# Another written order for the steps of a fused attention and SoLU kernel

## The chip, the cores and the metric

The kernel runs on one core of one Trainium2 chip. The metric is the device time of that core in microseconds (us): 400.5 us before, the median of three runs (400.12 to 400.53). The core has five engines that work side by side, each through its own queue in order: TensorE (PE in the profile; its weight loads PEld), VectorE (DVE), ScalarE (ACT), GpSimd (POOL) and SyncE (SP), which here issues all the transfers to and from memory.

## The reference

Packed attention for 8 batches of 8 heads, then a SoLU layer on the result:

```python
def sm_attn(qq, kk, vv):
    s = scale * np.matmul(qq, kk.transpose(0, 1, 3, 2))
    a = np.exp(s - np.max(s, axis=-1, keepdims=True))
    a = a / (np.sum(a, axis=-1, keepdims=True) + 1e-09)
    return np.matmul(a, vv)
p_packed = sm_attn(p, k, v)            # p: (8, 8, 32, 64), k, v: (8, 8, 576, 64)
out = sm_attn(q, p_packed, p_packed)   # q: (8, 8, 576, 64)
x = out.transpose(0, 2, 1, 3).reshape(4608, 512)
h = x @ w_in                           # w_in: 512 x 1024, float64
e = np.exp(h - np.max(h, axis=-1, keepdims=True))
solu = h * e / (np.sum(e, axis=-1, keepdims=True) + 1e-09)
mu = np.mean(solu, axis=-1, keepdims=True)
var = np.mean((solu - mu) ** 2, axis=-1, keepdims=True)
return ((solu - mu) / np.sqrt(var + 1e-06) * g_ln) @ w_out   # w_out: 1024 x 512, float64
```

## The kernel before

The work is cut into flows, each a Python generator. One step of a flow records the few instructions up to its next `yield`. The flows are:

- `Z`: warm-up matmuls on TensorE that feed nothing (L115, L117).
- loads, all issued by SP: `lw0` to `lw3` and `lo0` to `lo3` (1024 KB each, a quarter of w_in or of w_out, L168), `lg` (g_ln, L174), `lp` (p in two parts, 128 and 384 KB, L189), `lk`, `lq` and `lv` (one batch of k, q or v).
- `W0` to `W3` and `O0` to `O3` turn the float64 words of the weights into float32: a pass over the high words on ACT (L221), a shift on DVE (L223), a pass over the low words on ACT (L234), an add on POOL (L242, L254). `O` also sums squares on ACT (L251), for which it needs `g`, the transposed g_ln (PE L178, ACT L180). `S` and `C0` to `C7` split w_out into two fp16 parts `wch` and `wcl`.
- `p` transposes p on TensorE (L201) and copies it out on ACT (`pT`, L207).
- `k0` to `k7` (`pack`) make the packed attention of a batch: the transposed `kT`, scores (L385), exponentials (ACT L393), their transposes (L423, copied to `e1T` by ACT L425), the product with v (L433), and `ppT` (L440, L443). For batches 0 and 1, k and q are transposed by TensorE (L355, L361); for the later ones by DVE (L368).
- `q0` to `q7` (`unpack`) make the second attention of a batch: scores (L496, L505), softmax on all four engines, and the fp16 halves `a_h`, `a_l` (for batch 0 `a_r`, ACT L519 and DVE or POOL L521).
- `z0` to `z7` multiply the packed result by w_in (L565, L559) and split it into `zh`, `zl`. x @ w_in is then formed as attention weights times z.
- `t0` to `t35`: token tiles of 128 rows. A tile is 12 matmuls of 512 columns into `h` (L633; 24 of half height for a tile that lies across two batches), then max (DVE L636), exponential (ACT L654), product (DVE L658), centred halves `yhl` (ACT L664, DVE L666), a transpose by DMA (L669, `yT`), 24 matmuls of 512 columns with w_out (L688), a scaling (DVE L693) and the store (L695).

The steps run in the order of one string, and nothing reorders them afterwards:

```python
for name in ORDER.split():
    next(flows[name], None)
```

So the string sets, for each engine, the order of its queue. A load also waits for its buffer: `raw` has three, and `zh` and `zl` have two each, which first hold the raw words of weights. `LOAD_IN` says which weight goes where: lw2, lw0, lo1, lo3 into `zh`, lw1, lw3 into `zl`, lo0, lo2 into `raw`. A TensorE step that writes `h` waits for one of three pairs of PSUM banks.

Of the kernel before, what the change touches and what calls it, by code (L numbers as in the profile page):

```python
# [754 lines left out]
```

## Time and profile before

| | before |
|---|---|
| median of the runs | 400.5 us (400.12 to 400.53) |
| the profiled execution's own time | 401.95 us |
| its span, from the first to the last instruction | 400.2 us |
| PE busy | 383.8 us (96%) |
| DVE busy | 300.4 us (75%) |
| ACT busy | 259.4 us (65%) |
| POOL busy | 249.1 us (62%) |
| mean granted clock of TensorE | 0.983 |

The span is what can be read stage by stage. The profiled execution took 1.75 us more than its span and 1.45 us more than the median of the runs, so differences are carried from one to the other and not the totals. A busy share is a mean over the whole span; which engine sets the end has to be read from the stretches in which TensorE, the busiest, stands still.

### The profile page before, as it was taken

What the parts mean: (1) busy time and instruction counts of PE and PEld (TensorE: products, weight loads), DVE (VectorE), ACT (ScalarE), POOL (GpSimd) and SP (SyncE); (2) the same over time, 40 slices, a digit from 0 to 9 for tenths busy, and PEclk for the clock granted to TensorE, in tenths of its full rate; (3) what the DMA queues carried; (4) which work ended last, traced back from release to release, by engine and by line L of the source; (5) the groups of instructions that cost most, each with busy time, mean ns of one, the idle gap of its engine ahead of it and who ended that gap; (6) DMA issues with size and microseconds to landing.
All of it is one profiled execution on the core that took longest, in us unless ns stands there. A gap on an engine that the chain in (4) does not pass through costs nothing.

```text
span 400.2 us, 8803 instructions
## 1 busy us (share of the span) xinstructions
PE 383.8 (96%) x3370; PEld 202.3 (51%) x3370; DVE 300.4 (75%) x485; ACT 259.4 (65%) x443; POOL 249.1 (62%) x431
## 2 busy tenths in 40 slices
PE   8868699899999999999999999999999999999996
PEld 8746577453444544544445454444544444444444
DVE  0325779999799999987999767989886857755641
ACT  1677999984678657564648676666476577645440
POOL 1235779975448767675466657976576849854450
PEclk9978699999999999999999999999999999999999
DMA  8979999997799997889989957767554724436371
GB/s 277 405 255 363 224 197 116 214 169 142 132 201 163 172 168 203 166 147 160 213 175 195 223 119 138 139 138 197 109 96 99 118 68 103 106 79 131 80 157 52
DMA packets 213865, 66.11 MB, mean 165 GB/s; under 512 B 194744, under 2 KB 207808, under 8 KB 213312
## 3 DMA queue, kind: packets, MB, share of 16 engines
q1 hardware_dynamic: 213824, 65.56, 79.4%
q8 instruction: 26, 0.43, 0.5%
q14 instruction: 15, 0.12, 0.1%
HBM read 37.23 MB, written 9.44 MB: 117 GB/s over the span
## 4 chain that ended last, share of the span: by engine, by line
PE 82%; DMA 9%; ACT 3%; DVE 2%; SPq 1%; issue 1%; DVEq 0%; ACTq 0%
PE po L688 39%; PE h L633 23%; PE h L688 5%; DMA raw<-in_k_dram 5%; PE h L355 4%; DMA zh<-in_moe_w_in_dram 3%; PE h L385 3%; PE h L559 2%; PE h L505 2%; PE h L423 2%; PE pa L433 2%; DMA yT<-yhl 1%; ACT e L654 1%; DVE u L658 1%; SPq L151 1%
## 5 line engine op out<-in xcount | busy, mean ns | idle before, releaser
L688 PE MATMUL po<-wch,yT 128*128 128x512 f16 x512 | 159.3, 379 | 0.5 <-DMA yT<-yhl 0.5
L688 PEld LDWEIGHTS <-yT 128*128 128x128 f16 x888 | 85.9, 98 | 100.3 <-issue 3.8
L688 PE MATMUL po<-wcl,yT 128*128 128x512 f16 x256 | 97.0, 379 | 0.0
L658 DVE SCALAR_TENSOR_TENSOR u<-e,s_row,h 128x1024 f32<-128x1024 f32 x36 | 45.7, 1271 | 17.6 <-ACT e L654 11.2
L664 ACT ACTIVATE yhl<-u,negmu 128x1024 f16<-128x1024 f32 x36 | 41.2, 1148 | 27.1 <-POOL negmu L661 26.9
L636 DVE TENSOR_REDUCE nm<-h 128x1 f32<-128x1024 f32 x36 | 43.6, 1213 | 9.8 <-PE h L633 9.6
L666 DVE SCALAR_TENSOR_TENSOR yhl<-u,negmu,yhl 128x1024 f16<-128x1024 f32 x36 | 48.4, 1347 | 2.7 <-ACT yhl L664 2.5
L633 PE MATMUL h<-zl,a_h 128*128 128x512 f16 (+1 forms) x160 | 48.5, 381 | 0.0
L644 POOL TENSOR_SCALAR bound<-nm,z_scale 128x1 f32<-128x1 f32 x31 | 15.8, 511 | 44.7 <-DVE nm L636 39.7
L654 ACT ACTIVATE e<-h,nmc,z_scale 128x1024 f32<-128x1024 f32 x32 | 38.4, 1201 | 7.3 <-DVE nmc L639 6.6
L641 ACT ACTIVATE nmc<-nm,z_scale 128x1 f32<-128x1 f32 x29 | 8.5, 293 | 50.4 <-DVE nm L636 50.4
L672 ACT ACTIVATE e<-u,negmu 128x1024 f32<-128x1024 f32 x36 | 41.0, 1138 | 0.0
L633 PEld LDWEIGHTS <-a_h 128*128 128x128 f16 (+1 forms) x280 | 24.9, 101 | 30.7 <-issue 3.6
L693 DVE TENSOR_SCALAR o_sb<-po,c_row,inv 128x512 f32<-128x512 f32 x32 | 25.8, 808 | 19.3 <-PE po L688 16.3
L633 PE MATMUL h<-zh,a_h 128*128 128x512 f16 (+1 forms) x120 | 35.8, 380 | 0.0
L633 PE MATMUL h<-zl,a_l 128*128 128x512 f16 (+1 forms) x80 | 30.4, 380 | 0.0
L242 POOL TENSOR_TENSOR w_in_sb<-w_in_sb,u 128x1024 int32<-128x1024 int32 x4 | 9.5, 2379 | 26.2 <-ACT u L234 13.9
L680 POOL TENSOR_TENSOR c_row<-c_row,neg_half 128x1 f32<-128x1 f32 x36 | 22.9, 636 | 3.0
L633 PE MATMUL h<-zh,a_l 128*128 128x512 f16 (+1 forms) x60 | 22.7, 379 | 0.0
L355 PE MATMUL h<-ident,raw 128*64 128x128 f32 x256 | 19.6, 321 | 1.9 <-DMA raw<-in_k_dram 1.9
L650 POOL TENSOR_TENSOR s_row<-bound,neg_one 128x1 f32<-128x1 f32 x33 | 19.5, 592 | 2.7
L688 PE MATMUL h<-wch,yT 128*128 128x512 f16 (+1 forms) x80 | 20.4, 336 | 0.7 <-DVE o_sb L693 0.7
(174 smaller groups left out, 728.6 us busy)
## 6 DMA issues: line engine op xcount, KB each, us to landing
out_dram<-o_sb SPq DMA_DIRECT2D x35, 256.0 KB, 2.2
v_sb<-in_v_dram SPq DMA_DIRECT2D x8, 1024.0 KB, 6.2
raw<-in_k_dram SPq DMA_DIRECT2D x24, 288.0 KB, 5.0
raw<-in_q_dram SPq DMA_DIRECT2D x96, 72.0 KB, 2.8
zh<-in_moe_w_in_dram SPq DMA_DIRECT2D x2, 1024.0 KB, 9.1
raw<-in_k_dram SPq DMA_DIRECT2D x2, 1024.0 KB, 8.1
zl<-in_moe_w_in_dram SPq DMA_DIRECT2D x2, 1024.0 KB, 9.7
raw<-in_moe_w_out_dram SPq DMA_DIRECT2D x2, 1024.0 KB, 10.8
```

The costliest lines, as they stand in the source:

```text
L355: nc.tensor.matmul(pt[64 * r:64 * r + 64, g * MAIN + c * P:g * MAIN + (c + 1) * P], lhsT=rows[:, c, 2 * (g0 + g) + r], rhs=ident, start=Tr ...
L633: nc.tensor.matmul(dst_[:, cols], lhsT=lhsT, rhs=z[:, r, cols], start=bool(first), stop=bool(last))
L636: nc.vector.tensor_reduce(out=nm, in_=h, axis=AX.X, op=ALU.max, negate=True)
L650: nc.gpsimd.tensor_tensor(out=s_row, in0=bound, in1=neg_one, op=ALU.pow)
L654: nc.scalar.activation(e, h, AF.Exp, bias=nmc, scale=sc[:, 1:], accum_out=se)
L658: nc.vector.scalar_tensor_tensor(out=u, in0=e, scalar=s_row, in1=h, op0=ALU.mult, op1=ALU.mult, accum_out=su)
L664: nc.scalar.activation(yhl[:, 0], u, AF.Identity, bias=negmu)
L666: nc.vector.scalar_tensor_tensor(out=yhl[:, 1], in0=u, scalar=negmu, in1=yhl[:, 0], op0=ALU.add, op1=ALU.subtract)
L672: nc.scalar.activation(e, u, AF.Square, bias=negmu, accum_out=sq)
L680: nc.gpsimd.tensor_tensor(out=c_row, in0=c_row, in1=neg_half, op=ALU.pow)
L688: nc.tensor.matmul(po[:, cols], lhsT=yT[:, a, c], rhs=w[:, c, cols], start=c == 0 and t == 0, stop=c == NFC - 1 and t == 2)
L693: nc.vector.tensor_scalar(out=o_sb[:, cols], in0=po[:, cols], scalar1=c_row, scalar2=inv, op0=ALU.mult, op1=ALU.mult)
```

## The change

Only the string `ORDER` is another. It holds the same steps of the same flows, as often as before, so that every instruction is recorded with the same operands and sizes; where they stand in each engine's queue is what differs, and the order in which buffers go round follows from it. Nearly the whole string is another; its beginning:

```diff
-ORDER = 'Z lw2 lk0 lg lw1 W1 W1 k0 g W1 lp k0 lo0 g O0 k0 O0 k0 lp O0 lw3 W2 p lw0 p W1 k0 k0 lq0
+ORDER = 'lp lw1 lo0 W1 Z W1 p W1 lg lk0 lp g W1 O0 lw3 k0 O0 k0 lw2 g W3 p k0 p k0 lq0 k0 W3 W2 k0
...
```

The three places below are the ones that the steps of the next sections speak of.

**SP, the first loads of the program.** `zh`, `zl`, `raw` and `e` are the buffers that the weights, k, q and p are loaded into. Before:

```order
L168 DMA zh<-in_moe_w_in_dram 128x2048
L125 DMA raw<-in_k_dram 128x8x256
L139 DMA raw<-in_k_dram 64x4x64 x2
L174 DMA g_raw<-in_moe_g_ln_dram 8x128
L168 DMA zl<-in_moe_w_in_dram 128x2048
L189 DMA e<-in_p_dram 128x256
L168 DMA raw<-in_moe_w_out_dram 128x2x1024
L189 DMA e<-in_p_dram 128x3x256
L168 DMA zl<-in_moe_w_in_dram 128x2048
L168 DMA zh<-in_moe_w_in_dram 128x2048
L125 DMA raw<-in_q_dram 128x8x256
```

Now:

```order
L189 DMA e<-in_p_dram 128x256
L168 DMA zl<-in_moe_w_in_dram 128x2048
L168 DMA raw<-in_moe_w_out_dram 128x2x1024
L174 DMA g_raw<-in_moe_g_ln_dram 8x128
L125 DMA raw<-in_k_dram 128x8x256
L139 DMA raw<-in_k_dram 64x4x64 x2
L189 DMA e<-in_p_dram 128x3x256
L168 DMA zl<-in_moe_w_in_dram 128x2048
L168 DMA zh<-in_moe_w_in_dram 128x2048
L125 DMA raw<-in_q_dram 128x8x256
L139 DMA raw<-in_q_dram 64x4x64 x2
L168 DMA zh<-in_moe_w_in_dram 128x2048
```

In the order of the flows this was lw2, lk0, lg, lw1, lp, lo0, lp, lw3, lw0, lq0 and is now lp, lw1, lo0, lg, lk0, lp, lw3, lw2, lq0, lw0. In both the next loads are lo1, lv0, lo2, lo3, lk1 and lq1.

**ACT, its first passes, right behind the warm-up activation.** `e<-` is the pass over the high words of a weight (L221), `u<-` that over the low words (L234), named by the buffer that it reads; `zl` is w1 and then w3 in both. Before:

```order
L221 ACTIVATE e<-zl 128x1024
L234 ACTIVATE u<-zl,one_up 128x1024
L180 ACTIVATE g_sb<-po 128x8
L221 ACTIVATE e<-raw 128x1024
L357 COPY kT<-h 128x2x512
L251 ACTIVATE mag,ssq<-yT,g_sb 128x512
L221 ACTIVATE e<-zh 128x1024
L207 ACTIVATE pT<-h 128x512
L363 COPY kT<-h 128x2x2x64
L207 ACTIVATE pT<-h 128x512
L221 ACTIVATE e<-zh 128x1024
L234 ACTIVATE u<-zh,one_up 128x1024
```

Now:

```order
L221 ACTIVATE e<-zl 128x1024
L234 ACTIVATE u<-zl,one_up 128x1024
L221 ACTIVATE e<-raw 128x1024
L180 ACTIVATE g_sb<-po 128x8
L221 ACTIVATE e<-zl 128x1024
L207 ACTIVATE pT<-h 128x512
L357 COPY kT<-h 128x2x512
L221 ACTIVATE e<-zh 128x1024
L363 COPY kT<-h 128x2x2x64
L207 ACTIVATE pT<-h 128x512
L251 ACTIVATE mag,ssq<-yT,g_sb 128x512
L234 ACTIVATE u<-zh,one_up 128x1024
```

The first `e<-raw` (of o0) has moved ahead of `g_sb`, w3 (the second `e<-zl`) has come up to right behind it, and w2 is now the third weight of w_in instead of the second.

**DVE, the last rows ahead of `yhl` of tile 7 (its L666, the last row).** `kT<-raw` and `qT<-raw` are transposes of a later batch's k and q. Before:

```order
L482 TENSOR_REDUCE sm<-a_1633 128x18
L486 TENSOR_SCALAR sm<-sm 128x18
L487 RECIPROCAL sm<-sm 128x18
L368 STREAM_TRANSPOSE qT<-raw 128x576
L693 TENSOR_SCALAR o_sb<-po,c_row,inv 128x512
L413 TENSOR_SCALAR rs<-ssum 128x2
L414 RECIPROCAL rs<-rs 128x2
L368 STREAM_TRANSPOSE qT<-raw 128x576
L516 STREAM_TRANSPOSE s_1748<-a_1618 128x576
L666 SCALAR_TENSOR_TENSOR yhl<-u,negmu,yhl 128x1024
```

Now:

```order
L693 TENSOR_SCALAR o_sb<-po,c_row,inv 128x512
L413 TENSOR_SCALAR rs<-ssum 128x2
L414 RECIPROCAL rs<-rs 128x2
L368 STREAM_TRANSPOSE kT<-raw 128x576
L516 STREAM_TRANSPOSE s_1807<-a_1660 128x576
L368 STREAM_TRANSPOSE qT<-raw 128x576
L636 TENSOR_REDUCE nm<-h 128x1
L437 TENSOR_SCALAR pp<-pa,rs 128x64 x2
L368 STREAM_TRANSPOSE kT<-raw 128x576
L516 STREAM_TRANSPOSE s_1838<-a_1687 128x576
L666 SCALAR_TENSOR_TENSOR yhl<-u,negmu,yhl 128x1024
```

From `yhl` of tile 1 to that of tile 7 three more `kT` transposes, one more `qT` transpose and one more each of L516, L390 and L474 now stand in this queue.

## Rows read from the trace of the kernel before

**Rows 1.** The page, part 1: busy time, share of span and instructions.

```profile
PE 383.8 (96%) x3370; PEld 202.3 (51%) x3370; DVE 300.4 (75%) x485; ACT 259.4 (65%) x443; POOL 249.1 (62%) x431
```

**Rows 2.** Waits of PE from 58 us on: total us, times, longest.

```profile
PE h L385 <- ACT e L393: 0.8, 1, 0.8
...
PE h L505 <- DVE ppT L443: 0.7, 1, 0.7
PE po L688 <- DMA yT<-yhl: 0.5, 1, 0.5
```

**Rows 3.** Timeline of PE: start, us, operation, count [idle before <-releaser].

```profile
8.51 3.66 PE L117 MATMUL po<-ones 128*128 128x512 f32 x15
...
44.43 6.28 PE L355 MATMUL h<-ident,raw 128*64 128x128 f32 x64 [1.95 <-DMA raw<-in_k_dram]
...
53.41 3.71 PE L355 MATMUL h<-ident,raw 128*64 128x128 f32 x64
```

**Rows 4.** Timeline of ACT up to 57 us, the passes that waited.

```profile
12.17 1.17 ACT L221 ACTIVATE e<-zl 128x1024 f32<-128x1024 f32 x1 [9.95 <-DMA zl<-in_moe_w_in_dram]
...
15.17 1.19 ACT L221 ACTIVATE e<-raw 128x1024 f32<-128x1024 f32 x1 [0.61 <-DMA raw<-in_moe_w_out_dram]
...
22.86 1.12 ACT L221 ACTIVATE e<-zh 128x1024 f32<-128x1024 f32 x1 [2.18 <-DMA zh<-in_moe_w_in_dram]
...
33.45 1.01 ACT L425 COPY e1T<-h 128x1024 f32<-128x1024 f32 x1 [2.04 <-PE h L423]
...
56.58 0.69 ACT L519 CAST a_r<-s 128x576 fp32r<-128x576 f32 x1
```

**Rows 5.** Timeline of SP, three issues of loads: start, us.

```profile
0.72 0.40 SPq L168 DMA_DIRECT2D zh<-in_moe_w_in_dram  x1
...
8.97 0.34 SPq L168 DMA_DIRECT2D zl<-in_moe_w_in_dram  x1
...
25.12 0.39 SPq L168 DMA_DIRECT2D zh<-in_moe_w_out_dram  x1
```

**Rows 6.** The DMA view of those three issues: KB, us to landing.

```profile
zh<-in_moe_w_in_dram SPq DMA_DIRECT2D x1, 1024.0 KB, 4.9
zl<-in_moe_w_in_dram SPq DMA_DIRECT2D x1, 1024.0 KB, 11.2
zh<-in_moe_w_out_dram SPq DMA_DIRECT2D x1, 1024.0 KB, 5.1
```

**Rows 7.** Engines by stretch; last columns granted clock, DMA share, GB/s.

```profile
24.00:27.00 3.00, 0.67 (x8) 0.40 (x12) 1.36 (x2) 3.00 (x7) 1.83 (x1) 0.81 0.29 45
40.00:50.00 10.00, 6.99 (x83) 5.95 (x81) 7.47 (x10) 9.88 (x18) 7.42 (x5) 0.66 0.99 225
```

**Rows 8.** Groups of ACT and DVE by line and shape: busy us, mean ns.

```profile
L285 ACT ACTIVATE wch<-yhl,gs 128x512 f16<-128x512 f32 x4 | 2.9, 722 | 0.0
L641 ACT ACTIVATE nmc<-nm,plain 128x1 f32<-128x1 f32 x4 | 1.2, 288 | 0.1
L368 DVE STREAM_TRANSPOSE kT<-raw 128x576 f32<-128x576 f32 x24 | 17.9, 754 | 0.0
```

**Rows 9.** Timeline of PE where a fp16 block gives way to an fp32 one.

```profile
126.90 0.38 PE L688 MATMUL po<-wch,yT 128*128 128x512 f16 x1
127.20 0.47 PE L385 MATMUL h<-kT,pT 64*32 64x288 f32 x8
```

**Rows 10.** Tile 7: its transposing DMA on SP, its first L688.

```profile
138.13 3.27 SPq L669 DMA_TRANSPOSE yT<-yhl  x1
...
151.71 0.38 PE L688 MATMUL po<-wch,yT 128*128 128x512 f16 x1
```

**Rows 11.** The DMA view of the whole run: KB each, median us to landing.

```profile
raw<-in_k_dram SPq DMA_DIRECT2D x24, 288.0 KB, 5.0
...
yT<-yhl SPq DMA_TRANSPOSE x36, 4.4
```

**Rows 12.** Waits of DVE from 84 to 150 us.

```profile
DVE nm L636 <- PE h L633: 3.0, 1, 3.0
```

More of the change, by code (lines that the diff above doesn't have):

```diff
@@ new lines @@
+ORDER = 'lp lw1 lo0 W1 Z W1 p W1 lg lk0 lp g W1 O0 lw3 k0 O0 k0 lw2 g W3 p k0 p k0 lq0 k0 W3 W2 k0 p O0 W2 W2 W3 p k0 k0 p k0 lw0 k0 k0 W3 k0 q0 W0 p lo1 k0 O0 O0 p k0 q0 W2 W0 O1 q0 O0 W0 lv0 k0 O1 lo2 k0 k0 q0 q0 k0 k0 O1 O1 k0 q0 k0 k0 O2 q0 W0 lo3 z0 lk1 O2 z0 O1 lq1 q0 O2 O3 O1 q0 q0 q0 q0 z0 q0 O3 O2 q0 k1 q0 q0 q0 z0 q0 z0 z0 O2 O2 lk2 z0 O3 z0 q0 k1 k1 q0 q0 k1 k1 z0 O3 k1 q0 q0 z0 z0 lk2 S q0 z0 lk2 k1 z0 z0 q0 k1 S q0 k1 O3 q1 z0 lk2 q0 S q0 k1 q1 k1 lv1 lk3 q0 lk3 O3 q1 q0 C3 z0 C3 t0 C2 C2 q1 C4 t0 k2 C3 C4 C5 k1 t0 k2 k2 t1 k1 k1 lk3 C4 t0 k1 t0 k1 k1 t1 C6 C0 k1 C2 k1 C1 C5 q1 t1 t0 C5 t2 k1 C0 t0 lq2 t1 k2 q1 k1 t0 k1 t0 k1 t1 t0 C1 C1 C6 t2 q1 k1 C0 N C7 C7 q1 q1 t1 C7 t2 N lv2 t3 q1 q1 C6 q1 q1 t1 t3 N t2 k2 N t0 t0 t0 t3 t1 k2 k2 t1 k1 t1 t0 t2 q1 t2 t2 t0 q1 t0 t1 N q1 N z1 k2 q1 z1 t2 z1 k2 lk4 t1 z1 H z1 z1 k2 t1 q1 q1 t1 k2 z1 k2 t0 lq2 t1 q1 q1 k2 q1 t3 k2 q1 t1 q1 t3 z1 k2 q1 lq2 t3 z1 k2 t2 q1 z1 q1 q2 t1 z1 q1 t2 t2 q2 z1 lk3 z1 k2 k3 t3 t4 t4 lq2 t3 k2 t2 H t4 t2 lv3 q2 k2 q2 H k2 t2 k2 H t4 t2 H t5 t6 H t4 k2 t2 t5 t3 t3 t4 q2 lq3 H t3 t4 H t2 t4 k2 lq3 z2 z2 t5 q2 lq3 t4 t6 H t3 t5 t4 t6 q2 t3 t6 z2 t3 t5 t3 t6 z2 t5 t5 t3 q2 t4 z2 t7 t7 t4 t5 lk4 t4 k3 t3 k3 t5 t4 q2 t5 t6 lq3 z2 t7 t4 t7 k3 z2 q3 z2 q2 z2 k3 t7 q2 t6 q2 z2 t4 k3 k3 q3 q2 z2 q2 q3 k3 t5 q2 t7 lk4 t5 t5 z2 t5 t4 z2 q2 t6 lk4 q2 k3 t5 k3 t8 k4 t6 q2 t6 t5 q2 lk5 k3 k3 t6 k4 t5 q2 k3 k3 k3 t8 k3 z2 z2 z2 z2 t7 k3 q2 q2 q3 t8 lk5 k3 t8 k4 t6 k3 q2 q2 q2 t7 q2 t6 lk5 lq4 t6 k3 t7 t6 t8 k3 q3 k4 t8 t7 t8 t6 q3 q3 q3 q3 t7 k4 k3 t8 k3 t9 z3 q3 t9 z3 t7 t9 t7 q3 t7 t9 t6 t7 t10 q3 q3 t9 t9 k4 lq4 t8 t10 t8 lq4 t8 t9 z3 t7 k4 q3 q3 q3 lk6 t8 t9 t10 q3 t8 t10 q3 t8 t8 k4 t10 t9 t9 z3 t10 t8 t10 t7 t11 t10 lk5 k4 k4 t9 z3 t8 z3 lv4 t11 q3 q4 t11 q3 k4 t11 k5 q3 t9 q3 t9 z3 t11 t9 t9 k5 t11 z3 t11 q3 k4 k4 k4 t9 t12 k4 t11 t10 t12 k4 z3 q3 k5 z3 t9 k4 k5 k4 z3 q3 t10 lq4 t10 t12 t12 z3 lq5 q4 k5 k4 k5 t10 t12 z3 q4 t10 z3 q4 t10 t10 k4 lk6 t12 z3 t11 q3 t10 k5 q4 q4 z3 t12 q4 k4 q4 t12 k5 z3 t13 t13 q4 t11 t11 t10 t11 k4 t13 k5 t13 t13 t13 t11 t11 t13 t11 t14 t14 q4 q4 t12 t12 t12 t11 lv5 t13 t12 t11 t13 t12 t12 t12 t14 q4 lq5 q4 t15 q4 t15 t14 q4 t14 t14 t13 t14 t13 k5 t12 q4 t13 t13 t14 k4 q4 z4 t15 t12 lk6 t13 q4 q4 t13 t15 t15 t16 t13 t16 t15 t15 q5 q4 t14 t14 t14 z4 lk6 t14 t15 t14 t13 t16 q4 k6 t14 t14 t16 k5 lk7 k6 t16 lq5 t14 t15 q4 k6 k6 t16 z4 t15 k5 k5 t17 k5 q4 t17 k6 z4 t14 q4 lk7 t16 k5 z4 k5 lq5 z4 t16 t15 t16 k5 t17 k5 q4 t17 q5 t15 t15 q5 q5 t16 z4 t16 t15 k5 t17 t15 k5 q5 k6 t15 q4 z4 t17 z4 k5 z4 q5 k6 lk7 q5 z4 lk7 t15 t17 q5 k6 t16 q5 q5 t16 lq6 t16 z4 z4 z4 q5 z4 t17 q5 k6 z4 t16 z4 t17 t18 t18 t16 t17 q5 q5 t19 q5 q5 q5 t19 q5 k6 t17 t18 t16 t18 t19 t17 t18 t18 k5 lv6 t17 t17 lq7 t19 t19 t18 t17 t18 t21 t19 k6 k5 t19 lq6 t17 t18 t20 t18 z5 z5 q5 q5 t19 k6 k6 k6 k7 t21 t17 t20 z5 t18 k6 z5 t18 t18 k7 lq6 t18 z5 z5 t20 t20 t19 q6 t19 t21 q5 lq6 t18 t20 t20 k7 z5 z5 q6 t19 t20 t18 k6 z5 k6 t20 k6 t21 z5 z5 q5 q6 t19 z5 t18 t19 q5 k6 q5 t21 q6 q5 z5 k6 t19 t20 k7 z5 t19 t20 z5 z5 q6 q5 t21 z5 t19 k7 t21 t20 q6 q6 t21 q6 k6 t22 t22 t19 k6 t20 k6 t21 t22 t20 t22 t20 z6 k7 t20 t22 q6 t22 t20 t23 t22 t22 t20 k7 t21 lq7 t23 t21 t22 t21 t21 t23 t23 t21 z6 t23 z6 t21 q6 t22 t21 t24 t21 t23 t24 q6 t22 t22 t22 t23 t22 t23 lq7 t24 t24 t22 q6 z6 k7 t24 t23 t23 t22 lq7 q6 q6 t22 q7 t24 lv7 t24 k7 z6 t25 t23 z6 k7 q6 z6 z6 z6 t25 t24 t23 t24 t23 q6 q7 t25 t25 k7 q6 t25 t23 t24 t23 t23 z6 q6 q7 k7 q6 t25 t23 k7 t26 q6 t26 k7 t25 q6 t24 t25 z6 k7 z6 k7 k7 t26 q6 t26 k7 q6 q6 z6 t24 k7 z6 t25 q6 t24 z6 k7 t24 z6 q7 t26 t25 t26 q6 t26 z6 k7 t24 t24 q7 q7 t24 q7 q7 t26 t27 t25 t27 q7 t27 t26 q7 t25 t25 t25 t25 q7 q7 q7 t28 k7 q7 t25 t26 t28 t27 t27 t27 k7 t27 q7 t26 q7 t28 t26 t27 t26 z7 t28 q7 t26 t25 t27 t26 t27 q7 t27 z7 t29 z7 t26 t28 t29 z7 q7 q7 t27 t28 t28 t27 t26 t29 t27 t28 t27 z7 t28 t28 z7 t30 q7 t27 t28 t27 z7 t30 t29 q7 z7 q7 q7 q7 z7 t29 t29 z7 t29 t28 t30 t30 z7 t29 t30 z7 q7 t28 t28 z7 t28 z7 z7 t30 z7 t29 z7 t28 t29 t30 t29 t31 t28 t31 t31 t31 t29 t30 t29 t31 t31 t31 t29 t29 t29 t31 t30 t30 t30 t29 t32 t32 t30 t32 t32 t31 t32 t32 t30 t32 t30 t30 t31 t33 t33 t30 t31 t32 t31 t31 t31 t30 t31 t33 t33 t33 t31 t34 t33 t33 t33 t32 t34 t32 t35 t31 t32 t32 t34 t34 t35 t34 t33 t34 t34 t33 t35 t35 t32 t32 t33 t34 t32 t35 t33 t32 t35 t34 t33 t33 t35 t32 t35 t33 t35 t34 t33 t33 t35 t34 t34 t34 t34 t35 t34 t35 t34 t34 t35 t35 t35 t35 t35 t35 t35'
```

1 line of the change is left out of this document (removed).

## The prediction

> **What bounds the kernel now.** I read the page first: TensorE is busy for 383.8 of 400.2 us [rows 1], so only two kinds of time can be won, stretches in which TensorE stands still or runs at half clock, and I looked for where these lie. The view of waits shows that from 58 us on, which is where the first token tile enters TensorE, it hardly ever waits: 0.8 us for an exponential, 0.7 us for `ppT`, 0.5 us for a transposed tile [rows 2]. Nearly all the rest of the 16 us lies ahead of that. There TensorE works on attention of batches 0 and 1 in pieces, waits for loads and runs part of it at half clock: the granted clock averages 0.66 from 40 to 50 us [rows 7], and the 64 profiled rows of the k1 transpose take 6.28 us there against 3.71 us for the same rows of q1 later [rows 3]. So the end is set by when the token tiles can start, plus a TensorE queue that from then on is nearly full.
>
> What sets that start? In the timeline of ACT the reader is to see four waits ahead of the second `a_r` half at 56.58 us, the last softmax result that the first tiles need: 9.95, 0.61, 2.18 and 2.04 us, 14.8 in all [rows 4]. Three of them are for weights that have not landed, one is for TensorE. From 40 to 50 us ACT is busy for 9.88 of 10 us [rows 7]. So ACT is the engine that is late: it starts its weight passes at 12.17 us and then works through a queue. What a new order of the start is worth is how much less ACT waits in it.
>
> **The change, part 1: the first loads.** The time at which a load lands goes by the KB issued up to and with it. From issue and time to landing [rows 5, 6] or from the wait that it ended [rows 4] I have five marks of before: w2, 1024 KB, at 0.72 + 4.9 = 5.6 us; w1, 3200 KB (k0 is 1152), at 12.2; o0, 4352 KB (with the first 128 of p), at 15.2; w3, 5760 KB (with the other 384), at 8.97 + 11.2 = 20.2; w0, 6784 KB, at 22.9. The new order, read off between these marks: w1 at 1152 KB lands at 6.0 us, o0 at 2176 at 9.1, k0 at 3328 at 12.5, w3 at 4736 at 16.6, w2 at 5760 at 20.2, and w0 at 7936 (beyond the marks, at the slope of the last two) at 25.9.
>
> **Part 2: the queue of ACT on these loads.** ACT is free at 12.17 - 9.95 = 2.2 us. It waits 3.8 us for w1. Two passes of about 1.1 us [rows 4] end at 8.2. It waits 0.9 us for o0 and passes over it until 10.2. Next is `g_sb`, which needs a transpose on TensorE behind the warm-up, which ends at 8.51 + 3.66 = 12.2 us, and now behind a quarter of p: 16 rows of a shape that takes 3.71/64 each [rows 3], 0.9 us. So `g_sb` starts at 13.2, a wait of 3.0 us that before lay inside the wait for w1. Then w3: a wait of 3.2 us to 16.6. Its pass, a copy of `kT` (1.0, the length of the copy in [rows 4]) and one of p with half its columns (0.5) end at 19.2, and w2 costs 1.0 us more. Behind it stands work without a break: before w0 is needed ACT has some 6.5 us to do, to 26.8, and w0 is there by 25.9. The sum of waits is 3.8 + 0.9 + 3.0 + 3.2 + 1.0 = 11.9 us, 2.9 less than before. Bounds: if w2 follows w3 at the fastest pace between marks (2.6 us for 1024 KB), its wait goes to nothing and the saving is 3.8; if the wait for the transposed exponentials (2.04 us, behind q0 transposes at half clock) comes back, the saving is 0.9. I take 2.9, since ACT has two more weight passes queued ahead of the `e1T` copy as cover for that wait; without this cover it costs the 2.0.
>
> The load of o1 waits until ACT has read w2's low words out of its `zh` buffer; before, that came at 25.12 us [rows 5], and the transfers had run dry: 45 GB/s from 24 to 27 us [rows 7]. In the new order the same pass ends at about 23.9 us with w0 still under way, so that hole closes and v0, o2, o3 and k1 follow without it. I give nothing extra for this: ACT is already counted as busy there.
>
> **Part 3: what ACT does earlier.** Ahead of the `yhl` pass of tile 0 the new queue of ACT holds one more `wch` conversion (0.72 us) and one more `nmc` (0.29 us) [rows 8] than the old. That gives back 1.0. The start is earlier by 2.9 - 1.0 = 1.9 us (-0.1 to 2.8). TensorE has the same set of matmuls ahead of its first L633 in both orders and the same ahead of its first L688, so a start that is earlier by so much ends earlier by so much, unless it waits anew.
>
> **Part 4: the rest of the TensorE queue.** Counted in the order from the first L633 on, TensorE goes 45 times from fp16 work to fp32 work instead of 40. Such a passage costs 0.30 - 0.22 = 0.08 us more than a step within the block [rows 9], so 0.4; the way back is not priced by a row here, 0 to another 0.4, and I take 0. Between `h` of tile 2 and its L688 the new order has 25 us of other TensorE work instead of 18, so the 0.5 us wait for its transposed tile [rows 2] should go. For the other waits I assume no change. Sum: -1.9 + 0.4 - 0.5 = -2.0 us, from 401.95 to 399.95 us for the profiled execution and, carried over to the median of 400.5, **398.5 us**.
>
> **Rivals.** *Slower: VectorE is late at tile 7.* Between `yhl` of tiles 1 and 7 its queue holds three `kT` transposes and one `qT` transpose more, 0.754 us each [rows 8], and one more of L516, L390 and L474 over the same 576 columns, so some 5.3 us; and TensorE has 12 matmuls of 0.22 us, 2.6 us, less to do ahead of the tile's L688. Before, the tile's transposing DMA goes out at 138.13 [rows 10], needs 4.4 us [rows 11], and TensorE takes it at 151.71 [rows 10]: 9.2 us to spare. After, 1.3 us are left, if VectorE waits as little as before (3.0 us in one wait from 84 to 150 us [rows 12]). But four transposes that moved ahead of `yhl` each stand behind a load, and such a load takes 5.0 us [rows 11]. If VectorE stands for one of them, TensorE stops for 5.0 - 1.3 = 3.7 us: 402.2 us. It eats the gain from a delay of 1.3 + 2.0 = 3.3 us on. Against it: no wait for a load is among VectorE's before. It gets 0.22, with all smaller new waits.
>
> *No change: the start gains nothing.* The saving at ACT is at its lower bound, or POOL and VectorE, which also stand in the chain to the first tile, hand nothing on. Then the start costs 0.1 more, and 0.1 + 0.4 - 0.5 leaves 400.5 us. For it speaks that ACT still has the same passes to do before the first tile. A second way to the same end is that the weights do not land one by one. The waits show w1, o0 and w0 in the order of their issue [rows 4]. The Trainium skill, DMA: Bandwidth & Descriptors, section Queues, rings and completion order, says that completion is not first-in-first-out per issuing engine, since each transfer runs on several rings that finish independently; the trace agrees in so far as w3 took 11.2 us, more than its place in the sequence explains. As a mechanism of this kernel: if w3 lands only together with w2, at 20.2 us, ACT waits 3.8 + 0.9 + 3.0 + 6.8 = 14.5 us, the saving is 0.3, and the sum gives 401.1 us. Together 0.16.
>
> *Faster than forecast: the start is worth its upper bound* of 2.8 us and the two other waits of [rows 2] go too: 400.5 - 2.8 + 0.4 - 2.0 = 396.1 us. For it speaks the closed hole in the transfers, against it that nothing in the new order aims at those waits. 0.10.
>
> **How the numbers follow.** The forecast case has 0.52, with a range of its own of 396.8 to 399.6. Within 0.2% of 400.5, that is 399.7 to 401.3, I call no change; a measurement of this kernel can hardly tell less. Faster is 0.52 + 0.10 = 0.62, same 0.16, slower 0.22. The range must leave out no more than 2 in 10: it goes from 395.4, a little under the fast rival, to 402.4, just over the slow rival's price.
>
> **What would show it.** In the changed profile ACT's first L221 starts at about 6 us, the wait ahead of `g_sb` is near 3 us, the waits ahead of the second `a_r` half sum to about 12 us, and that half, behind 1.4 us more of other passes than before, starts at about 55 us. The first L688 on TensorE comes some 2 us earlier than before, and its waits from there on stay under 2 us. The prediction is wrong if w1 or w3 lands much later than 6.0 and 16.6 us, if ACT shows a new wait over 1 us between 27 and 54 us, or if TensorE waits for `yT` of tile 7 or of any later tile.

## The result, and the profile after

The changed kernel takes 402.74 us, the median of 14 runs (401.31 to 405.68); the kernel before takes 401.09 over its 14 runs here. The ratio of the runs is 1.0056 [1.0037, 1.0074]: slower by 0.56%, some 2.25 us (the two medians alone lie 1.65 us apart), where 398.5 us was predicted. Eight of the 14 runs lie from 401.31 to 402.80 us and six from 403.98 to 405.68; the profiled execution, 404.76 us with a span of 402.9 us against 400.2, is one of the six, so its trace can show more loss than the median has.

Two rows cut the span: the first L633, where the first token tile enters TensorE, and the last matmul. Before, they start at 58.17 and 396.71 us, 338.5 us apart. After, in the timeline of PE:

```profile
58.58 0.50 PE L633 MATMUL h<-zh,a_r 128*128 128x512 f32 x1
...
399.47 0.27 PE L688 MATMUL h<-wch,yT 128*128 128x256 f16 x1
```

They are 340.9 us apart. So of the 2.7 us that the span grew, 0.4 lie ahead of the first tile, where 1.9 were to be won, and 2.4 behind it, where nothing was to change much. I call the two parts the start and the rest.

**The start.** The timeline of ACT up to the second `a_r` half, the passes that waited (answers to [rows 4]; in brackets the wait and what ended it):

```profile
7.10 1.17 ACT L221 ACTIVATE e<-zl 128x1024 f32<-128x1024 f32 x1 [4.89 <-DMA zl<-in_moe_w_in_dram]
...
9.87 1.14 ACT L221 ACTIVATE e<-raw 128x1024 f32<-128x1024 f32 x1 [0.45 <-DMA raw<-in_moe_w_out_dram]
...
14.17 0.18 ACT L180 ACTIVATE g_sb<-po 128x8 f32<-128x8 f32 x1 [3.16 <-PE po L178]
...
17.63 1.16 ACT L221 ACTIVATE e<-zl 128x1024 f32<-128x1024 f32 x1 [3.28 <-DMA zl<-in_moe_w_in_dram]
...
20.68 1.14 ACT L221 ACTIVATE e<-zh 128x1024 f32<-128x1024 f32 x1 [0.50 <-DMA zh<-in_moe_w_in_dram]
...
37.56 1.12 ACT L221 ACTIVATE e<-raw 128x1024 f32<-128x1024 f32 x1 [1.53 <-DMA raw<-in_moe_w_out_dram]
...
48.61 0.31 ACT L484 ACTIVATE sm<-sm,eps 128x18 f32<-128x18 f32 x1 [0.38 <-DVE sm L482]
...
53.57 0.74 ACT L393 ACTIVATE e<-h,nmx 128x576 f32<-128x576 f32 x1 [0.38 <-DVE nmx L390]
...
56.85 0.69 ACT L519 CAST a_r<-s 128x576 fp32r<-128x576 f32 x1
```

The reader is to see that the first five waits sum to 12.3 us, with 11.9 predicted, each within 1.1 us of its term, and that three waits behind them, 2.3 us, were not foreseen; the largest is for o2 at 37.56 us. The sum, 14.6, is close to that of before (14.8), and `a_r` comes at 56.85 instead of 56.58.

TensorE in the same stretch (answers to [rows 3]):

```profile
34.44 2.39 PE L433 MATMUL pa<-v_sb,e1T 128*32 128x64 f32 x80 [2.06 <-DMA v_sb<-in_v_dram]
...
43.70 3.71 PE L355 MATMUL h<-ident,raw 128*64 128x128 f32 x64 [0.32 <-DMA raw<-in_k_dram]
...
50.59 0.39 PE L260 MATMUL pa<-ssq,ones_f 128*128 128x8 f32 x2 [1.79 <-ACT mag L251]
...
52.65 2.98 PE L355 MATMUL h<-ident,raw 128*64 128x128 f32 x32
```

The k1 transpose is now at full speed, 3.71 us instead of 6.28. But a wait of 2.06 us for v0 and one of 1.79 us for ACT are new, and so is a slow L355 (32 rows in 2.98 us). The windows view (columns as in [rows 7]) shows the clock and the loads:

```profile
24.00:27.00 3.00, 0.98 (x18) 0.98 (x20) 0.84 (x2) 3.00 (x6) 1.44 (x1) 1.00 0.74 220
40.00:50.00 10.00, 7.50 (x118) 4.47 (x106) 7.50 (x12) 9.62 (x18) 7.65 (x4) 0.94 1.03 220
...
34.00:41.00 7.00, 5.50 (x114) 3.25 (x117) 2.75 (x6) 5.44 (x11) 3.01 (x2) 0.52 1.05 371
51.00:55.00 4.00, 4.00 (x40) 2.83 (x42) 3.15 (x11) 3.59 (x8) 2.64 (x3) 0.57 1.40 140
```

The hole in the transfers from 24 to 27 us is closed (220 GB/s, 45 before), and from 40 to 50 us the clock is 0.94 instead of 0.66. The stretches near half clock (1.2 of 2.4 GHz) now stand at 34 to 41 and 51 to 55 us (before: 26 to 33 and 43 to 50, at 0.52 each), each begun around one of TensorE's waits. All in all TensorE is busy 1.2 us less ahead of the first L633 than before (47.1 us, 48.25 before) and stands 1.6 us longer (11.5 against 9.9). And the transfers as a whole are hardly ahead: 331 GB/s over the first 40 us against 325 before, 0.24 MB.

**The rest.** The page's part 1 and the waits of PE from 60 us on (answers to [rows 1, 2]):

```profile
PE 383.3 (95%) x3370; PEld 200.5 (50%) x3370; DVE 301.1 (75%) x485; ACT 260.1 (65%) x443; POOL 250.4 (62%) x431
```

```profile
PE po L688 <- DMA yT<-yhl: 1.6, 1, 1.6
PE pa L433 <- ACT e1T L425: 1.1, 2, 0.8
PE pa L440 <- DVE pp L437: 0.7, 1, 0.7
PE h L633 <- DVE s L470: 0.5, 1, 0.5
PE h L505 <- DVE ppT L443: 0.3, 1, 0.3
```

TensorE is busy as long as before (383.3 against 383.8 us), so the longer span is standing still. The waits sum to 4.2 us. Those of [rows 2], with one of 0.2 us for `s` that they don't show, sum to 2.2. (One of 0.7 us for `o_sb`, near the end, is in both and left out of both sums.) So 2.0 of the rest's 2.4 us are waits. The 0.4 left is as much as five further crossings into fp32 were priced at, but counted in the two traces from the first L633 on these go from 47 to 50, three more, which by the same price is 0.2; no run tests them alone. The old waits for the exponential (0.8) and for tile 2's `yT` (0.5) are gone; the new ones stand in three places: tile 1 (84.76), batch 2's packed attention (93.08), and tile 7 (142.91, 149.77).

### The profile page after: what moved, and what is told of

It reads as the page before. It is cut to its first block, busy times and chain, and to the rows that moved or that the text cites. A ratio compares the mean times of both kernels' runs of the same rounds, so it can differ in the third digit from the quotient of the medians.

```text
span 402.9 us, 8802 instructions
## 1 busy us (share of the span) xinstructions
PE 383.3 (95%) x3370; PEld 200.5 (50%) x3370; DVE 301.1 (75%) x485; ACT 260.1 (65%) x443; POOL 250.4 (62%) x431
## 4 chain that ended last, share of the span: by engine, by line
PE 79%; DVE 8%; DMA 6%; ACT 2%; SPq 2%; issue 1%; DVEq 0%; ACTq 0%
PE po L688 39%; PE h L633 23%; PE h L688 5%; DMA zh<-in_moe_w_in_dram 3%; DMA v_sb<-in_v_dram 2%; PE h L559 2%; PE pa L433 2%; PE h L385 2%; PE h L505 2%; DVE nm L636 1%; PE h L355 1%; SPq L139 1%; DMA raw<-in_k_dram 1%; PE h L423 1%; DVE u L658 1%
## 5 line engine op out<-in xcount | busy, mean ns | idle before, releaser
L688 PE MATMUL po<-wch,yT 128*128 128x512 f16 x512 | 158.7, 379 | 1.6 <-DMA yT<-yhl 1.6
L688 PEld LDWEIGHTS <-yT 128*128 128x128 f16 x888 | 85.8, 98 | 102.4 <-issue 4.5
L688 PE MATMUL po<-wcl,yT 128*128 128x512 f16 x256 | 97.0, 379 | 0.0
L666 DVE SCALAR_TENSOR_TENSOR yhl<-u,negmu,yhl 128x1024 f16<-128x1024 f32 x36 | 48.3, 1341 | 5.2 <-ACT yhl L664 5.2
L633 PE MATMUL h<-zl,a_h 128*128 128x512 f16 (+1 forms) x160 | 48.5, 381 | 0.0
L633 PEld LDWEIGHTS <-a_h 128*128 128x128 f16 (+1 forms) x280 | 24.8, 101 | 31.4 <-issue 3.3
L633 PE MATMUL h<-zh,a_h 128*128 128x512 f16 (+1 forms) x120 | 35.8, 380 | 0.5 <-DVE s L470 0.5
L633 PE MATMUL h<-zl,a_l 128*128 128x512 f16 (+1 forms) x80 | 30.4, 380 | 0.0
L644 POOL TENSOR_SCALAR bound<-nm,z_scale 128x1 f32<-128x1 f32 x31 | 10.6, 341 | 31.6 <-DVE nm L636 29.0
L661 POOL TENSOR_SCALAR negmu<-su 128x1 f32<-128x1 f32 x36 | 8.6, 238 | 27.7 <-DVE u L658 25.7
L633 PE MATMUL h<-zh,a_l 128*128 128x512 f16 (+1 forms) x60 | 22.7, 379 | 0.0
L489 POOL TENSOR_TENSOR a<-a,sm 128x576 f32<-128x576 f32 x16 | 18.5, 1162 | 5.1 <-DVE sm L487 4.9
L688 PE MATMUL h<-wch,yT 128*128 128x512 f16 (+1 forms) x80 | 20.6, 337 | 0.7 <-DVE o_sb L693 0.7
```

The lines of the kernel that those rows point to most:

```text
L489: EN(nc, SOFT_BY[2 * b + 1]).tensor_tensor(out=w2, in0=w2, in1=sm.unsqueeze(2).broadcast_to([P, NB, J]), op=ALU.mult)
L633: nc.tensor.matmul(dst_[:, cols], lhsT=lhsT, rhs=z[:, r, cols], start=bool(first), stop=bool(last))
L644: by.tensor_scalar(out=bound, in0=nm, scalar1=-1.0 / U_MAX, scalar2=sc[:, :1], op0=ALU.mult, op1=ALU.max)
L666: nc.vector.scalar_tensor_tensor(out=yhl[:, 1], in0=u, scalar=negmu, in1=yhl[:, 0], op0=ALU.add, op1=ALU.subtract)
L688: nc.tensor.matmul(po[:, cols], lhsT=yT[:, a, c], rhs=w[:, c, cols], start=c == 0 and t == 0, stop=c == NFC - 1 and t == 2)
```

## The experiments

Each is the order of one kernel with a few steps moved. Each ratio is to runs of the kernel before that were taken beside it, whose median goes from 400.94 to 402.08 us. A diff shows steps of the string; `...` is what stands as it was. "Rest" is the time from the first L633 to the last matmul, as above: 338.5 us before, 340.9 after.

**Start and rest apart.** One order was taken up to a step, and the steps that were left then follow as they stand in the other.

```diff
 e1_start_new: the new order up to the cut, then the old one
 ... q1 q0 C3 z0 C3 | C2 C2 C4 k2 t0 k1 ...
 e2_rest_new: the old order up to the cut, then the new one
 ... k1 C4 z0 k2 | lk3 C3 C3 t0 q1 t0 ...
 e4_new_from_tile7: the old order up to the first step of t7, then the new one
 ... t3 q2 lk5 | lk4 t6 t6 t6 t7 ...
```

> New order up to the first step of tile 0, old order from there on. In the two traces the change is 0.4 us late at the first L633, 1.6 us at 103 us and 2.8 us at the end. Theory A (the start is worth nothing either way, the loss lies in the steps behind the first tile): ratio to before 0.998 to 1.002, the waits from 60 us on those of before. Rival B (the start is to blame, since it hands the tiles their inputs late): 1.004 to 1.006, with the waits for yT near 84 us and for pp near 143 us still there.

Measured: 400.31 us, ratio 0.9987 [0.9974, 0.9999]; first L633 at 56.85, rest 337.9.

> Old order up to the first step of tile 0, new order from there on. Theory A: 1.004 to 1.006, since the waits for yT at tile 1 (1.6 us), e1T (0.8 us) and those from 140 to 150 us (1.2 us) belong to the new rest. Rival B: 0.999 to 1.001.

Measured: 403.97 us, ratio 1.0066 [1.0048, 1.0085]; rest 339.4 in its profile, which is of one of the shortest of its runs (402.52 us; they go from 402.51 to 404.66). The wait for yT at tile 1 (1.6 us) and one for e1T (0.6) are there; from 120 to 155 us, where 1.2 us of waits were expected, there is none.

> Old order up to the first step of tile 7, new order from there on. By theory A about 1.2 us of the loss lie behind 103 us: 1.002 to 1.004 if they belong to the steps behind this place, among them the wait at 140 to 150 us. If the wait there comes from steps ahead of this place, or from being late at 103 us, 0.999 to 1.001. Rival C (the 45 passages of TensorE from fp16 to fp32 work instead of 40 are what costs): the loss is spread over the whole queue, 1.003 or more, with no wait over 0.5 us.

Measured: 404.71 us, ratio 1.0109 [1.0078, 1.0140]. That is none of the three outcomes. The seam brings waits that stand in neither whole order (1.2 us for `o_sb` at 130 us, 0.4 for `zf`), so it says nothing clean on tile 7.

What follows, by the ratios: the new start is worth 0.5 us and the new rest costs 2.65 us; 2.15 together, against 2.25 measured for both. The loss is in the rest.

**The start: is it the load of v0, or k1?** In the changed kernel TensorE waits 2.06 us for v0. One kernel loads it earlier; one leaves most of it out. But the order alone does not bring that wait. In e1, which has the same order up to there, the matmul waits for ACT, and the timelines of PE and of ACT read:

```profile
34.27 1.45 PE L433 MATMUL pa<-v_sb,e1T 128*32 128x64 f32 x80 [0.56 <-ACT e1T L425]
```

```profile
37.09 1.19 ACT L221 ACTIVATE e<-raw 128x1024 f32<-128x1024 f32 x1 [1.06 <-DMA raw<-in_moe_w_out_dram]
```

So it is in g1, g2, g3, h1 and h3 below, which have this start too: the wait for v0 is 0.19 us at most, that at L260 0.43, the clock from 34 to 41 us 0.88 to 1.00 and from 51 to 55 us 1.00; the k1 transpose takes 4.97 to 5.38 us instead of 3.71. What all seven traces have is ACT's wait for o2, of 0.56 to 1.53 us.

```diff
 f1_v_load_early: the changed kernel with
-... q0 W0 p lo1 ... q0 O0 W0 lv0 k0 O1 lo2 ...
+... q0 W0 p lv0 lo1 ... q0 O0 W0 k0 O1 lo2 ...
```

> The change with one step moved: the load of v0 goes ahead of the load of o1, which stands until ACT has read w2. In the change TensorE waits 2.06 us at L433 for v0, and then runs half of its matmuls from 34 to 41 us at half clock. If that wait is what ate the gain of the start, L433 starts near 32.5 us instead of 34.4, ACT's wait for o2 (1.53 us) shrinks with it, and the time falls by 1.5 to 2.5 us, to 0.999 to 1.002 of before. If TensorE only waits elsewhere for the same softmax passes of ACT, the time is that of the change, 1.004 to 1.007.

Measured: 405.71 us, ratio 1.0123 [1.0105, 1.0141], worse than either range; first L633 at 59.18. The wait for v0 is gone and another of its size stands at the same matmul. The timelines of ACT and of PE:

```profile
33.27 1.17 ACT L221 ACTIVATE e<-zh 128x1024 f32<-128x1024 f32 x1 [1.63 <-DMA zh<-in_moe_w_out_dram]
```

```profile
36.77 1.32 PE L433 MATMUL pa<-v_sb,e1T 128*32 128x64 f32 x80 [2.08 <-ACT e1T L425]
```

The pass over o1, which now lands later, stands ahead of the copy of `e1T` on ACT. A load that is moved up moves another down.

```diff
 x1_v0_one_head: the changed kernel with
-nc.gpsimd.memset(v_sb[LEFT:, H * W * D:], 0.0)
+nc.gpsimd.memset(v_sb, 0.0)
 and, in the load of v for batch 0, 128 of the 1024 KB; the other batches whole
```

> The change with the load of v0's main part cut to one head of eight (128 of 1024 KB; the other heads are zeros, so the attention result of batch 0 is not the reference's), all instructions on the other engines as in the change, but for the memset of the whole of v_sb. Theory D (the start is bound by the bytes that have to land, some 13 MB in its first 40 us, whatever their order): o2 lands 2.5 to 3 us earlier, the waits of ACT for o2 (1.53 us) and of TensorE for v0 (2.06 us) go, the first L633 starts at 55.5 to 57 us instead of 58.6, and the time falls by 1.5 to 2.5 us against the change. Rival (ACT's queue of passes bounds the start): ACT's waits go but the second half of a_r and the first L633 move by less than 0.7 us.

Measured: 402.24 us, ratio 1.0010 [0.9989, 1.0032]; first L633 at 56.73. The waits for o2 and v0 are gone, and `a_r` comes at 56.11 us, as in e1 (56.24), where v0 is whole. Freed of these, ACT waits for TensorE and k1 is waited for 1.9 us. By the time theory D's forecast came: the ratio is 0.46%, some 1.8 us, under the changed kernel's. By the trace it is not shown: the first L633 is 0.1 us ahead of e1's, and a start that has v0 whole is as early. So the two late loads don't decide the start alone, and where x1's 1.8 us come from stays open; that the changed kernel's other runs waited for v0 as its profiled one did, and x1's never, would explain it, but they have no trace.

```diff
 all three: e1 with
 h2_k1_ahead_of_o3:
-... W0 lo3 z0 lk1 ...
+... W0 lk1 lo3 z0 ...     and O3 O3 moved to ... O2 O3 O2 O3 lk2 ...
 h3_ppT_first:
-... C5 C7 t0 t2 k1 ...
+... C5 C7 k1 t0 t2 ...
 h4_k1_and_ppT: both
```

> New start and old rest, with the load of k1 ahead of that of o3, and ACT's and VectorE's first pass over o3 some 3 us later to match. In the run with the new start and the old rest the load of k1 goes out at 33.5 us, since it stands on the queue behind the load of o3, which waits until ACT has read w0; TensorE waits 1.4 us for k1, to 43.3 us, and runs the 64 rows of L355 at half clock for part. Theory E (k1's landing sets the start): k1 goes out near 30.5 us, L355 starts at 41.9 us, the first L633 comes 1 to 3 us earlier than 56.85, ratio to before 0.992 to 0.997. Rival (ACT's queue up to the second half of a_r sets it): L355 starts earlier, TensorE waits as long for a copy of ACT behind it, the first L633 moves by less than 0.5 us, 0.998 to 1.000.

> New start and old rest, with k1's copy of ppT (L443) ahead of tile 0's second pass (L666) on VectorE. In the old rest TensorE waits 0.7 us for ppT at L505, since VectorE is in L666 for 2.27 us. If the wait goes and tile 0's transposed tile is still in time (5 us to spare), the time falls by 0.6 to 0.8 us: 0.996 to 0.9975 of before. If tile 1 is late for it, 0.998 to 1.000.

> Both of the two runs ahead of this in one kernel. By theory E and a wait that stands for itself, the gains add up: 0.990 to 0.996 of before. If the earlier start only makes the next wait longer, as good as the better one of the two.

Measured: h2 405.76 us, ratio 1.0112 [1.0094, 1.0129], first L633 at 61.52; h3 400.85, 0.9993 [0.9978, 1.0008]; h4 405.82, 1.0118 [1.0099, 1.0136]. In h2 k1 is there early and the first tile 4.7 us later than in e1. Its timeline of PE, and its window from 45 to 61 us:

```profile
41.75 3.71 PE L355 MATMUL h<-ident,raw 128*64 128x128 f32 x64
...
48.73 1.94 PE L565 MATMUL h<-w_in_sb,ppT 64*32 64x512 f32 x16 [2.90 <-ACT kT L357]
```

```profile
45.00:61.00 16.00, 11.99 (x120) 7.05 (x116) 10.54 (x18) 13.27 (x26) 9.97 (x7) 0.68 1.30 179
```

k1's landing came as theory E has it, the price did not. TensorE finishes k1's rows early at full clock and stands 2.90 us for ACT's copy of them, as the rival has it; with that wait the clock from 45 to 61 us averages 0.68. In e1 the same rows start at 43.30, take 5.38 us, and the next wait is 0.43. In h2 the copy stands on ACT behind a square of o3, which waits 0.87 us for VectorE's pass over o3; these passes were moved with the load, so h2 does not test k1's landing alone. h3 turned a wait of 0.7 us into two of 0.3 and 0.2, and gained nothing that can be told.

```diff
 h5_k1_copy_first: e1 with k1's copy on ACT ahead of o3's squares, S on TensorE behind k1's scores
-... z0 O3 k1 q0 ... lk2 S q0 z0 lk2 k1 z0 ...
+... z0 k1 O3 q0 ... lk2 q0 z0 lk2 k1 S z0 ...
```

> New start and old rest, with two steps of the start moved: on ACT k1's last copy of kT (L363) goes ahead of the last square of w_out (L251, 0.9 us), and on TensorE k1's first scores (L385) ahead of the matmul that sums these squares (L260). In the run without the moves TensorE waits 0.43 us at L260 and starts L385 at 50.8 us, as soon as that copy is done, and is busy from there to the first L633 at 56.85 us. Theory F (the order of ACT's passes around k1's copies sets the start): L385 starts near 49.9 us, the first L633 0.7 to 1.0 us earlier, ratio to before 0.996 to 0.998, if a_r (second half at 56.24) is in time for it. Rival (a_r or the first conversions of w_out are next in line): the first L633 comes earlier but TensorE stands in it or at the first L688, 0.998 to 1.000.

Measured: 401.34 us where the kernel before took 402.08, ratio 0.9985 [0.9970, 1.0000]; first L633 at 57.10. No better than e1: TensorE now waits 0.21 us for `a_r` inside the first tile.

**The rest: are the three places its loss?** Each place was mended by moving steps of the changed kernel.

```diff
 g1_tile1: the scaling of w_out's sixth part (POOL) ahead of tile 2's step
-... C7 t2 N lv2 t3 q1 q1 C6 q1 ...
+... C7 C6 t2 N lv2 t3 q1 q1 q1 ...
 g2_tile7: k4's two transposes (DVE L368) behind k3's pp
-... t5 k3 t8 k4 t6 ... k3 k3 t6 k4 t5 ... lk5 k3 t8 k4 ...
+... t5 k3 t8 t6 ... k3 k3 t6 t5 ... lk5 k3 k4 k4 t8 k4 ...
 g3_both: both
 h1_k2_chain: g3, and on ACT k2's exponential ahead of a copy of z1, its e1T ahead of tile 3's exponential
-... z1 H z1 z1 k2 t1 ... q1 k2 q1 t3 k2 q1 ... z1 k2 q1 lq2 ...
+... z1 H z1 k2 z1 t1 ... q1 k2 q1 k2 k2 t3 q1 ... z1 q1 lq2 ...
```

> The change with one step moved: GpSimd's last conversion of w_out (L293, 1.16 us) goes ahead of the bound of tile 2, so that it no longer runs beside VectorE's second pass over tile 1 (L666), which took 2.04 us there against 1.27 us before. Theory A (the pass is drawn out by GpSimd's, tile 1's transposing transfer goes out later by that, and TensorE stands for it): L666 takes about 1.3 us, the wait of TensorE for tile 1 falls from 1.57 to about 0.8 us, the time by 0.8 us or 0.2%: 1.003 to 1.005 of before. If the pass stays long, or if the transfer itself is late because of others on its queue, the wait stays at 1.6 us and the time at that of the change.

Measured: 402.25 us, ratio 1.0021 [1.0002, 1.0040], a little faster than theory A's range. Its profile is of one of its longest runs (403.93 us), with a rest of 341.5. The wait for tile 1 shrinks and two of the next place grow (timeline of PE):

```profile
82.61 0.39 PE L688 MATMUL po<-wch,yT 128*128 128x512 f16 x1 [0.33 <-DMA yT<-yhl]
...
87.32 1.23 PE L423 MATMUL h<-ident,e 128*128 128x128 f32 x8 [0.65 <-ACT e L393]
...
92.06 1.32 PE L433 MATMUL pa<-v_sb,e1T 128*32 128x64 f32 x80 [0.98 <-ACT e1T L425]
```

> The change with two steps moved: the first two block transposes of k4 (L368), which stand behind its load, go on VectorE from ahead of k3's last scaling (L437) to behind it. Theory A (VectorE stands for the load and what TensorE needs stands behind it): pp of k3 comes some 2.5 us earlier, the waits of TensorE at L440 (0.7 us) and for s (0.5 us) go, and where the trace of the change loses 1.8 us between tile 7 and tile 8 it loses 0.3 to 0.6; the time falls by 1.2 to 1.5 us: 1.001 to 1.003 of before. Rival: VectorE has the same work to do and the next in line is late in its place, tile 7's second pass or tile 8's, and the time stays within 0.1% of the change, 1.005 to 1.006.

Measured: 403.07 us, ratio 1.0035 [1.0020, 1.0049]; between the two forecasts. The wait for `pp` is gone, that for `s` (0.5) and that of 1.6 us at tile 1 stand. Its runs lie within 1.7 us, those of the changed kernel within 4.4.

> Both moves of the two runs ahead of this together. If the two places are the loss behind the first tile, their gains add up: 2.0 to 2.3 us less than the change, 0.999 to 1.001 of before; what is then left against the kernel with the new start and the old rest (0.9987) is the 0.4 us for five more passages between fp16 and fp32 work. If the loss only moves on to the next place, 1.003 to 1.006.

Measured: 402.49 us, ratio 1.0022 [1.0008, 1.0036]: between the two forecasts, and no better than g1. Batch 2's attention took up part of what tile 1 gave: in its trace L433 waits 0.98 us (0.60 in g2's) and L423 0.41 (none in g2's). Its rest is 340.5.

> On top of both moves (tile 1 and tile 7): on ACT the exponential of k2's second half goes ahead of a copy that waits 2.0 us for VectorE (L596), and the small copy of k2's transposed exponentials goes ahead of tile 3's exponential. In the run with both moves TensorE waits 0.4 us at L423 and 1.0 us at L433 for these two between 86 and 92 us, waits that came up when tile 1's wait was taken away. If each wait of the new rest stands for itself, both go, and the time falls by 1.0 to 1.4 us against both moves: 0.9985 to 1.000 of before. If VectorE and ACT are simply behind TensorE in this stretch, the wait moves to tile 3 or to tile 4's a_h, and the time stays within 0.1% of both moves (1.0022).

Measured: 400.89 us, ratio 0.9994 [0.9979, 1.0010]; rest 338.8. Its waits of PE from 60 us on:

```profile
PE h L505 <- DVE ppT L443: 0.7, 1, 0.7
PE h L633 <- DVE s L470: 0.5, 1, 0.5
PE po L688 <- DVE z_scale L334: 0.4, 1, 0.4
PE pa L433 <- ACT e1T L425: 0.3, 1, 0.3
```

They sum to 1.9 us against 4.2, and of the 0.66% that e2 puts on the new rest 0.62 are back (1.0056 to 0.9994). So the three places are the loss of the rest, as nearly as intervals of 0.15 to 0.19% to either side can tell.

```diff
 h6_all_moves: h1 with the two moves of h5
```

> The same two moves on top of the change with its three places mended behind the first tile (tile 1, k2, tile 7), which gave 0.9994. Theory F: 0.997 to 0.9985, under before and with all of the new order but some ten steps. Rival: 0.999 to 1.0005.

Measured: 401.06 us where the kernel before took 402.08, ratio 0.9975 [0.9963, 0.9988]; first L633 at 57.09, rest 339.0. It is the only one that beats the kernel before by more than 0.2%, and it beats the changed one by 0.8%, with the new start and the mended new rest. Beside h1 that is 0.19% less time, which h5's two moves alone (0.9985 against e1's 0.9987) don't explain; the intervals overlap.

## Why the prediction was wrong

**Where TensorE's time lies: too much was put ahead of the first tile.** Of the 16 us in which it is not busy in the kernel before, 9.9 lie there, 3.2 from there to the last matmul and 3.2 behind it.

**The landings and ACT's first queue: right to some 1 us.** The marks gave w1 6.0, w3 16.6 and w2 20.2 us; the passes that waited for them began at 7.10, 17.63 and 20.68. The wait ahead of `g_sb` was 3.16 us (3.0 predicted). In e1, g1, g3 and h3 the five waits sum to 11.9 to 12.1 us (11.9 predicted). w3 was there 3 us ahead of w2, so the way to no change by which the two land together did not happen; the weights that ACT waited for landed in the order of their issue. (The 11.2 us of w3 in the kernel before, taken as a sign of that way, are only 0.5 us more than the line between o0's and w0's marks gives.)

**"Behind it stands work without a break": failed.** The sum stopped at w0, where the marks stopped. Carried on at their last slope (5.7 us for 2176 KB), o2, at 11136 KB in the new order, would land at 25.9 + 3200 · 5.7 / 2176 = 34.3 us. It landed at 37.56, and v0, 1024 KB ahead of it, was waited for until 34.44. The closed hole let the loads behind it start earlier, but they ran in a stream that was only 0.24 MB ahead at 40 us. So the rival that the start gains nothing describes the changed kernel's own profile, though not by the waits it named: ACT's saving was made (2.5 us of the 2.9, 14.8 - 12.3), and lost to the waits behind it. In e1, where v0 is in time, ACT still waits 1.9 us behind w2, 1.06 of it for o2 and the rest for TensorE.

How much the start is worth is e1's 0.13%, 0.5 us instead of 1.9. `a_r` comes at 55.98 to 56.71 us in the six other traces of this start, where about 55 was predicted, and the first L688, which was to come some 2 us earlier than before (76.52 us), starts at 76.22 in the changed kernel and at 75.31 in e1. Of the seven kernels with the whole new start unchanged, after, e1, g1, g2, g3, h1 and h3, six have their first L633 between 56.60 and 57.33 us, and the changed kernel's profiled execution at 58.58; the three with the old start up to there (before, e2, e4) have it between 57.13 and 58.17. What holds it at some 57 us was not settled. Three chains end there within about 1 us of each other: ACT's passes (`a_r` at 56 to 57), k1, which SP issues behind o3 and which lands at 43 to 44, and TensorE at half clock after its waits. f1, x1, h2 and h5 each pulled at one, and another held.

**"For the other waits I assume no change": failed, and it decided the sign.** It is the term of the sum that cost most: 2.0 us more waiting in the trace, where 0.5 less was counted. The end of tile 2's wait (-0.5) was right; the crossings (+0.4) are not tested. What was not read is how little slack the steps that feed TensorE had. At tile 1 two starts that lie 0.2 us apart decided. The timelines of DVE, POOL, SP and PE before:

```profile
77.21 1.27 DVE L666 SCALAR_TENSOR_TENSOR yhl<-u,negmu,yhl 128x1024 f16<-128x1024 f32 x1
```

```profile
77.43 2.07 POOL L293 TENSOR_TENSOR wcl<-yhl,wch 128x512 f16<-128x512 f32 x1
```

```profile
78.55 1.93 SPq L669 DMA_TRANSPOSE yT<-yhl  x1
```

```profile
83.48 0.39 PE L688 MATMUL po<-wch,yT 128*128 128x512 f16 x1
```

and after:

```profile
77.51 2.04 DVE L666 SCALAR_TENSOR_TENSOR yhl<-u,negmu,yhl 128x1024 f16<-128x1024 f32 x1
```

```profile
77.31 1.16 POOL L293 TENSOR_TENSOR wcl<-yhl,wch 128x512 f16<-128x512 f32 x1
```

```profile
79.58 2.09 SPq L669 DMA_TRANSPOSE yT<-yhl  x1
```

```profile
84.76 0.39 PE L688 MATMUL po<-wch,yT 128*128 128x512 f16 x1 [1.57 <-DMA yT<-yhl]
```

The operation that starts first takes its own time and the other some 0.8 us more. Before, the other was POOL's, and TensorE shows no wait there; now it is `yhl`. Its transposing DMA goes out at 79.58 instead of 78.55, and TensorE, which is free for the tile at 84.76 - 1.57 = 83.2 us, about when it took it before (83.48), stands for it. The Trainium skill, SBUF — State Buffer, section SBUF: two separate sides, says that VectorE and GpSimd share one pair of ports as an exclusive lock, which whichever of a VectorE operation with two inputs in SBUF and a GpSimd operation that reads SBUF starts first holds for its whole instruction, while the other is blocked. The trace agrees in both directions: POOL's took 0.91 us more where `yhl` had 1.05 us left to run, and `yhl` 0.77 us more where POOL's had 0.96 left. Nor is it of one execution: `yhl` takes 2.01 to 2.04 us in e2, f1, x1 and g2 too, and TensorE stands 1.56 to 1.59 us for it. In g1 POOL's operation ends ahead of `yhl`, which takes 1.29 us, and the wait falls to 0.33; in g3 and h1 it is much the same (1.28 us, and 0.35 and 0.37).

**The slower rival: its mechanism came, its place and price did not.** That its 402.2 us lie near the 402.74 measured is luck. VectorE does stand for a load ahead of tile 7, and `yhl` is late (timeline of DVE):

```profile
135.86 0.78 DVE L368 STREAM_TRANSPOSE kT<-raw 128x576 f32<-128x576 f32 x1 [1.00 <-DMA raw<-in_k_dram]
...
142.31 0.46 DVE L437 TENSOR_SCALAR pp<-pa,rs 128x64 f32<-128x64 f32 x2
...
144.03 2.14 DVE L666 SCALAR_TENSOR_TENSOR yhl<-u,negmu,yhl 128x1024 f16<-128x1024 f32 x1
```

But TensorE stood for batch 3's `pp` (0.70) and for `s` (0.46), not for tile 7's `yT`; 1.2 us instead of 3.7. The rival asked only who waits for the tile, and not who waits for what stands between. g2 took this wait away by moving the two transposes behind `pp`. Whether this load is late varies: SP's issue of it took 2.00 us in the changed kernel and 0.43 in e2, where `pp` is in time. The timeline of DVE in e2:

```profile
134.78 0.78 DVE L368 STREAM_TRANSPOSE kT<-raw 128x576 f32<-128x576 f32 x1 [0.29 <-DMA raw<-in_k_dram]
```

f1, x1 and g1, which leave this place as it is, go with the changed kernel: an issue of 1.98 to 2.24 us, 1.08 to 1.25 us of VectorE for the load, 0.7 to 0.9 of TensorE for `pp`. The profiles of the changed kernel, x1 and g1 are of longer runs of theirs and that of e2 of a short one. That the late load makes the wide spread of the changed kernel's runs, and its mending the narrow one of g2, fits this but is not shown: most of g2's runs lie between the changed kernel's two groups and not in the lower one. Why the issue takes longer stays open. What tile 1 showed comes again here: `yhl` of tile 7 takes 2.14 us where GpSimd's L521 started first (143.82 us), and 1.24 in e2, where `yhl` did (142.36 against 142.82).

Mending tiles 1 and 7 (g3) brought back 0.34 of the 0.66%, and moving batch 2's exponential and `e1T` forward on ACT (h1) another 0.28. In g1's trace mending tile 1 alone hands most of its wait on to that chain. By its runs g1 gains as much as g3 all the same (0.35%), and g2 alone 0.21%, so how the 0.34% divides between tiles 1 and 7 is not settled.
